# Local and pooled attention into a mixture of experts: a new order, a shorter pooling matrix, sums on a second engine

## The chip, the cores and the metric

One Trainium2 chip, one core of it. The metric is the device time of one execution in microseconds (us); lower is better. The runs of a kernel are given by their median.

## The reference, cut to what matters

Two layers, all in float32. The first works on 8 images (batch) x 8 heads, sequence 576, head size 64; the second on the result as 8 x 576 rows of 512 features, with 4 experts of 64 columns, of which each row uses 2.

```python
def _attn_ref(q, k, v):                       # factor = 4
    q_d, k_d, v_d = means over 4 neighbours of q, k, v        # 144 positions
    out_d = sm_attn(q_d, k_d, v_d)
    out_up = np.repeat(out_d, factor, axis=2)
    mask = np.abs(pos[:, None] - pos[None, :]) < factor       # a band of 7
    ...
    attn = attn / (np.sum(attn, axis=-1, keepdims=True) + 1e-09)
    out_local = np.matmul(attn, v)
    return out_up + out_local

def _moe_ref(x, w_gate, wq, wk, wv, wo):      # K = 2
    logits = x @ w_gate
    w = softmax over the two largest logits of a row
    for e in range(4):
        q, k, v = x @ wq[e], x @ wk[e], x @ wv[e]
        a = causal softmax of (q @ k.T) / 8
        ye = a @ v @ wo[e]
        out += w (where e is among the two) * ye
```

## The kernel before, in words

For each image b the kernel runs three stages; stages of neighbouring images overlap (image b's first stage runs beside the second of b-1 and the third of b-2).

Stage 1 works on pairs of heads c = 0..3 of image b. `load` (L475) brings q, k (128 x 584, transposed) and v (two loads of 64 rows, five windows of 128). `s1_local` (L493) makes ten tiles of local scores on TensorE (PE), L505, masks them on VectorE (DVE), L508, takes maxima, L511, subtracts them on GpSimd (POOL), L520, exponentiates on ScalarE (ACT), sums, L523, adds epsilon to the sum, L524 (`l_eps`), takes the reciprocal and normalises, L526, on POOL or DVE. `s1_down` (L530) pools q and k by four (`down4`: one reduction on DVE, L541, with a piece of 16 columns more for k, or two additions on POOL, L545), pools v, makes the pooled scores (L578), their maxima (`d_max`), the scaling of the maxima by 1/128 (`d_scl`, L583), the exponential (L588), the sum with epsilon (`d_eps`, L591) and the normalisation (`d_nrm`). v is pooled in two ways: for image 0 by matmuls with a pooling matrix `pool` (L563), for the other images by additions (`vd`, L557 and L558, POOL or DVE) on a second copy of v, `lr`, that comes with two loads of its own, a large one (L484, 256 KB) and a small one (L486, 64 KB: 16 rows of 2 KB, read twice, for the two halves of 32 partitions). `s1_out` (L614) transposes both softmax results (L361), evicts them (L316 on DVE, L314 on ACT), multiplies with v (L643 to L655), adds both parts into x (L663, on DVE) and splits x into a high and a low part, xh (L668, ACT) and xl (L669). x(b,c) below is the result of pair c of image b.

Stage 2 projects x to q, k (L686; L701 for the first q) and v with the gate's logits (L732, L741), each as three products of high and low parts. Stage 3 makes causal scores by rows of two tiles (L845), maxima (L865), exponentials (L868), the sum with epsilon (`s_eps`, L872), the reciprocal (L873), the normalisation with the gate's weight (`s_nrm`, L876), transposes, products with v (L959) and the output projection (L982, L1004).

The order of the work is written out by hand as a list. Each operation that the functions above declare with `op(name, engines, cost, ...)` has a number; SEQ (L17 to L158) lists the numbers in the order in which the operations are issued. An entry x stands for operation x // 4, and x % 4 says which of the operation's engines does it: "GV" with remainder 0 is POOL, with 1 DVE. An entry -1 is a warming matmul on zeros (`filler`, L463), whose result nothing reads. There are 22 of them, and seven more at the start (L343). Each engine, and the queue of SyncE (SP) that issues all DMAs, does its part of the list strictly in order.

Buffers are slots of pools. In `load`, q and k have NLD = 2 slots each and v has NLV = 2, so the load of pair 2 waits until the last reader of pair 0 is through: for q the local scores and the pooling, for v the product with v. A load that waits holds all that stand behind it on SP. The tags "q" (NQ = 3 slots) and "k" (NK = 2) hold the projected q and k of stage 3, "xh" and "xl" (8 slots each) the two parts of x.

`constants` (L391) makes the pooling matrix `pool` (128 x 7 x 128): entry (row, k, column m) is 1 where the row's position lies in the group of four that column m stands for. It counts positions less four times the column with six counters on POOL (L398, L400; 704 columns in all), compares with 0 on DVE (L405) and with 3.5 (L410, L412), the second comparison multiplied by the first. `own` masks rows that belong to another window.

## Time and profile before

| | us |
|---|---|
| median of 3 runs | 457.26 (456.78 to 457.70) |
| the profiled execution, its own time | 456.31 |
| its span, first to last instruction | 454.5 |
| busy: PE, DVE, ACT, POOL | 442.4 (97%), 373.5 (82%), 335.2 (74%), 303.8 (67%) |

The profiled execution's time is 1.8 us more than its span (what lies around the first and last instruction), and 0.95 us less than the median of the runs. Busy time of PE is modelled at the ends of matmuls, so a full PE in a stretch says that a matmul follows a matmul, not that none could be faster. Idle time of an engine counts only where something behind it waits.

### The profile page before, as it was taken

To read this page: it belongs to the slowest core of one execution; us is meant where nothing else is said; L and a number is where in the kernel's file an instruction comes from. 1 tells how busy PE (TensorE), PEld (TensorE's weight loads), DVE (VectorE), ACT (ScalarE), POOL (GpSimd) and SP (SyncE) were. 2 spreads that over 40 slices of the span, in tenths; PEclk is the share of its full clock that TensorE was granted. 3 is DMA by queue.
4 is the path that set the end of the run, shared out by engine and by line. 5 is a ranking of instruction groups with operands and counts; after the bars stand their busy time and mean duration, and the time that the engine had idled before them with its cause. 6 is when DMAs were issued, how large, how long until landed. Compare 5 with 4: busy or idle time off the path is not lost.

```text
span 454.5 us, 20339 instructions
## 1 busy us (share of the span) xinstructions
PE 442.4 (97%) x8373; PEld 400.6 (88%) x8373; DVE 373.5 (82%) x1099; ACT 335.2 (74%) x1056; POOL 303.8 (67%) x447
## 2 busy tenths in 40 slices
PE   8889999999999999999999999999999999999997
PEld 3768998989999889999999898999898998999876
DVE  7989999899968999777889999996897658466782
ACT  2988797876968988766866886675997688366873
POOL 7789779769757988755893888855687861024340
PEclk9999999999999999999999999999999999999999
DMA  8787455343415542624354253333352200110112
GB/s 246 233 231 188 128 168 173 88 147 100 133 48 169 179 129 72 190 85 112 105 152 158 85 126 82 126 112 99 117 162 81 74 1 3 53 53 14 48 61 105
DMA packets 43460, 52.70 MB, mean 116 GB/s; under 512 B 3304, under 2 KB 26344, under 8 KB 43368
## 3 DMA queue, kind: packets, MB, share of 16 engines
q1 hardware_dynamic: 43368, 51.40, 38.1%
q8 instruction: 66, 1.08, 1.0%
q14 instruction: 26, 0.21, 0.2%
HBM read 40.90 MB, written 9.44 MB: 111 GB/s over the span
## 4 chain that ended last, share of the span: by engine, by line
PE 81%; DVE 10%; ACT 3%; issue 2%; DMA 2%; POOL 1%; SPq 0%; DVEq 0%; POOLq 0%; ACTq 0%
PE pj L686 20%; PE po L982 10%; PE sq L845 9%; PE pv L732 8%; PE o L959 8%; PE tq L361 5%; PE tp L361 4%; PE o L643 3%; PE sc L505 3%; PE scd L578 2%; PE pv L741 2%; PE po L1004 1%; PE o L650 1%; DMA lk<-in_kT_dram 1%; DMA lv<-in_v_dram 1%
## 5 line engine op out<-in xcount | busy, mean ns | idle before, releaser
L876 POOL TENSOR_SCALAR pr<-pr,pst,gt 128x128 f32<-128x128 f32 (+8 forms) x101 | 71.5, 718 | 51.3 <-DVE pst L873 33.0
L868 ACT ACTIVATE pr<-pr,pst 128x448 f32<-128x448 f32 (+8 forms) x144 | 79.9, 558 | 11.7 <-DVE pst L865 11.1
L686 PE MATMUL pj<-xh,wqk_h 128*128 128x320 f32 (+1 forms) x248 | 75.1, 303 | 0.0
L686 PE MATMUL pj<-xl,wqk_h 128*128 128x320 f32 (+1 forms) x248 | 73.2, 295 | 0.2 <-issue 0.2
L686 PE MATMUL pj<-xh,wqk_l 128*128 128x320 f32 (+1 forms) x248 | 72.9, 294 | 0.0
L865 DVE CUSTOM_DVE_ANT_0 pr<-sq,causal_t 128x448 f32<-128x448 f32 (+8 forms) x144 | 64.1, 484 | 5.1 <-PE sq L845 4.9
L845 PE MATMUL sq<-k,q 64*64 64x256 f32 (+6 forms) x768 | 51.8, 371 | 0.5 <-ACT k L314 0.5
L686 PEld LDWEIGHTS pj<-xh,wqk_h 128*128 128x128 f32 x248 | 46.6, 188 | 3.3 <-issue 1.1
L686 PEld LDWEIGHTS pj<-xh,wqk_l 128*128 128x128 f32 x248 | 46.6, 188 | 0.0
L686 PEld LDWEIGHTS pj<-xl,wqk_h 128*128 128x128 f32 x248 | 46.6, 188 | 0.0
L588 ACT ACTIVATE dp<-scd,dst 128x144 f32<-128x144 f32 x96 | 35.1, 375 | 9.9 <-DVE dst L583 7.3
L845 PEld LDWEIGHTS sq<-k,q 64*64 64x64 f32 x768 | 32.9, 133 | 7.9 <-ACT k L314 0.7
L526 POOL TENSOR_TENSOR lp<-lp,lst 128x640 f32<-128x640 f32 x25 | 32.4, 1294 | 8.5 <-DVE lst L525 6.0
L732 PE MATMUL pv<-wvg_h,xh 128*128 128x260 f32 x128 | 36.9, 288 | 0.2 <-ACT dp L588 0.2
L669 POOL TENSOR_TENSOR xl<-x,xh 128x576 fp32r<-128x576 f32 x23 | 32.8, 1425 | 5.1 <-ACT xh L668 5.1
L732 PE MATMUL pv<-wvg_l,xh 128*128 128x260 f32 x128 | 36.2, 283 | 0.0
L732 PE MATMUL pv<-wvg_h,xl 128*128 128x260 f32 x128 | 36.0, 282 | 0.0
L982 PE MATMUL po<-oh,wo_h 128*128 128x256 f32 (+1 forms) x112 | 34.0, 304 | 0.0
L971 POOL TENSOR_TENSOR ol<-oc,oh 128x256 fp32r<-128x256 f32 (+1 forms) x27 | 22.4, 830 | 16.2 <-ACT oh L970 16.0
L982 PE MATMUL po<-oh,wo_l 128*128 128x256 f32 (+1 forms) x112 | 32.9, 294 | 0.0
L982 PE MATMUL po<-ol,wo_h 128*128 128x256 f32 (+1 forms) x112 | 32.9, 294 | 0.0
L361 PE MATMUL tq<-ident,pr 64*128 64x64 f32 x736 | 32.3, 227 | 0.5 <-DVE ptb L316 0.5
(181 smaller groups left out, 1432.1 us busy)
## 6 DMA issues: line engine op xcount, KB each, us to landing
lv<-in_v_dram SPq DMA_DIRECT2D x64, 160.0 KB
lq<-in_qT_dram SPq DMA_DIRECT2D x32, 292.0 KB
lk<-in_kT_dram SPq DMA_DIRECT2D x32, 292.0 KB
out_dram<-ot SPq DMA_DIRECT2D x28, 288.0 KB
lr<-in_v_dram SPq DMA_DIRECT2D x28, 256.0 KB
lr<-in_v_dram SPq DMA_DIRECT2D x28, 64.0 KB
wst<-in_wqk_dram SPq DMA_DIRECT2D x1, 1024.0 KB
vx<-vg SPq DMA_DIRECT2D x8, 128.0 KB
```

Source lines behind the costliest of these rows:

```text
L361: T.transpose(ps()[:, 512 * x + z[x]:512 * x + z[x] + 64], data[r, 0:128], ident[r, r])
L526: op("l_nrm", "GV", (pool_tt(n), dve(n)), lambda e: eng[e].tensor_tensor(p(), p(), st[:, :, 2:3].to_broadcast([128, NT, W]), op=OP.mult), ...
L588: A.activation(p()[:, t, :], scs()[:, at * t:at * t + SD], AF.Exp, bias=st[:, t, 4:5], scale=1.0 / 128.0, accum_out=st[:, t, 0:1])
L669: op("xl", "GV", (1360, dve(576)), lambda e: eng[e].tensor_tensor(xl(), x(), xh()[:, 0:S].bitcast(F32), op=OP.subtract), r=[x, (xh, 0)], w ...
L686: T.matmul(ps()[:, H0 + n0:H0 + n1], ww[:, c, w0 + 128 * p:w0 + 128 * p + 128], xx[b, c]()[:, n0:n1], start=(i == 0), stop=(i == 3 * NP - 1))
L732: T.matmul(ps()[:, at:at + 260], xx[b, c]()[:, 128 * t:128 * t + 128], ww[:, c, :], start=(i == 0), stop=(i == 3 * NP - 1))
L845: T.matmul(pss[x][0]()[halves[e ^ turned(t)], at_of[x] + at + to:at_of[x] + at + to + n1 - n0], q()[r, 64 * t:64 * t + 64], k()[r, n0:n1], ...
L865: op("s_max", "V", dve(n) + 4, lambda x=x, t=t, n=n, src=src: V.tensor_tensor_reduce(rows_of[t], src(), causal_t[:, S - 64:S + 256] if t = ...
L868: op("s_exp", "A", 281 + n / 1.2, lambda x=x, t=t, n=n: A.activation(rows_of[t], rows_of[t], AF.Exp, bias=st[:, x, 4:5], scale=-1.0, accum ...
L876: op("s_nrm", "GV", (327 + n / 1.2 + max(0, n - 384) * 1.1, 189 + n / 1.92), lambda g, x=x, t=t, n=n: eng[g].tensor_scalar(rows_of[t], row ...
L959: T.matmul(obs[x]()[r, q0:q1], vg()[kr, j, 64 * (2 * p + e):64 * (2 * p + e) + 64], pt()[kr, e, j, q0:q1], start=j == 0, stop=j == len(job ...
L982: T.matmul(ps()[:, H1 + n0:H1 + n1], ww[:, p, 128 * c:128 * c + 128], xx[b, p]()[:, n0:n1], start=(i == 0), stop=(i == 5))
```

## The change

1. SEQ is new: 2591 entries for 2561, with 24 warming matmuls for 22. PE's part of the list has the same operations; from 80 us on they stand in the old order but for neighbours and near neighbours that change places. At the start the eleven warming matmuls before and after the first local tile are gone, and ten stand behind the first pooled scores. DVE's, ACT's and POOL's parts are new throughout. SP issues q and k of pairs 0 to 3 of image 0 ahead of most of v.
2. Sums with epsilon may go to POOL, as one addition of two columns; 49 of 128 do (24 `s_eps`, 15 `d_eps`, 10 `l_eps`). The scaling `d_scl` may go to ACT; 20 of 32 do. Pooling of q and k in image 1 and `d_nrm` in images 0 and 1 may now choose their engine as elsewhere. Over the whole list the engines of other operations change too, among them three more of the pooled values `vd` on DVE (13 for 10), six fewer poolings of k on POOL (11 for 17), three fewer xl on DVE (6 for 9), seven fewer evictions `tp_ev` on DVE (13 for 20).
3. Pairs 2 and 3 of image 0 are loaded into slots of the tags "q", "k" and "xh".
4. The pooling matrix comes from a row of column numbers (128 columns), and, for each row and each of the seven k, one number: the position shifted right by two, as a float. Column m belongs to the row where both are equal.
5. The small load of `lr` is two loads of 16 partitions each, each with one reading of the rows. This makes 28 more DMAs.

```diff
-    1152, 36, 2100, 20, 0, 193, -1, -1, -1, -1, -1, 4, 8, 16, 156, 196, -1, 32, 144, 292, 40, 140, 84, 88, 96, -1,
...
+    44, 0, 20, 24, 1168, 192, 2132, 32, 4, 156, 16, 197, 28, 208, -1, 212, 217, 36, -1, 140, 144, 292, -1, -1, -1,
...
+    def add_eps(e, dst, st):
+        if e == "G":
+            G.tensor_tensor(dst, st[:, :, 0], st[:, :, 1], op=OP.add)
+        else:
+            V.tensor_reduce(dst, st[:, :, 0:2], op=OP.add, axis=AX.X)
+
...
     def constants():
-        cks = [buf(wk, [128, n], "ck", 8, I32, tag="xh") for n in (512, 192)]
-        ges = [buf(wk, [128, n], "ge", 8, tag="xl") for n in (512, 192)]
+        row, at = buf(wk, [128, 128], "row", 8, I32, tag="xh"), buf(wk, [128, 2, 8], "at", 8, I32, tag="xl")
...
         def count():
+            G.iota(row(), pattern=[[1, 128]], base=0, channel_multiplier=0)
...
-                for ck, z0, z1, k0 in ((cks[0], 0, 512, 0), (cks[1], 0, 128, 4)):
-                    G.iota(ck()[r, z0:z1].rearrange("p (k m) -> p k m", m=128), pattern=[[TQ, (z1 - z0) // 128], [-4, 128]],
-                           base=TQ * k0 - PADL - 4 * WT + SH * x, channel_multiplier=1)
-                G.iota(cks[1]()[r, 128:192].rearrange("p (k z m) -> p k z m", z=2, m=WT), pattern=[[TQ, 2], [0, 2], [-4, WT]],
-                       base=-PADL + SH * x, channel_multiplier=1)
-
-        def above():
-            for x, n0, n1, own_x in ((0, 0, 512, 0), (1, 0, 128, 1), (1, 128, 192, 0)):
-                V.tensor_scalar(ges[x]()[:, n0:n1], cks[x]()[:, n0:n1], 0.0, own[:, own_x:own_x + 1], op0=OP.is_ge, op1=OP.mult)
+                G.iota(at()[r, 0, 0:5], pattern=[[TQ, 5]], base=SH * x - PADL - 4 * WT, channel_multiplier=1)
+                G.iota(at()[r, 0, 5:7], pattern=[[TQ, 2]], base=SH * x - PADL, channel_multiplier=1)
+
+        def group():
+            V.tensor_scalar(at()[:, 0, 0:7], at()[:, 0, 0:7], 2, None, op0=OP.arith_shift_right)
+            V.tensor_copy(at()[:, 1, 0:7].bitcast(F32), at()[:, 0, 0:7])
...
         def fill_pool():
-            flat = pool.rearrange("p k m -> p (k m)")
-            for x, n0, n1 in ((0, 0, 512), (1, 512, 640)):
-                V.scalar_tensor_tensor(flat[:, n0:n1], cks[x]()[:, 0:n1 - n0], 3.5, ges[x]()[:, 0:n1 - n0], op0=OP.is_lt, op1=OP.mult)
-            z = [t()[:, 128:192].rearrange("p (k m) -> p k m", m=2 * WT) for t in (cks[1], ges[1])]
-            V.scalar_tensor_tensor(pool[:, 5:7, 64 - WT:64 + WT], z[0], 3.5, z[1], op0=OP.is_lt, op1=OP.mult)
+            for k in range(7):
+                dst, src = (pool[:, k], row()) if k < 5 else (pool[:, k, 64 - WT:64 + WT].rearrange("p (z m) -> p z m", m=WT), strided(row()[:, 0:WT], (0, 2)))
+                own_x = own[:, 1:2] if k == 4 else own[:, 0:1]
+                V.tensor_scalar(dst, src, at()[:, 1, k:k + 1].bitcast(F32), own_x, op0=OP.is_equal, op1=OP.mult)
...
         def masks():
...
-        op("c_cnt", "G", 2100, count, w=cks, alloc=cks)
-        op("c_ge", "V", 740, above, r=cks, w=ges, alloc=ges)
-        op("c_pool", "V", 1430, fill_pool, r=cks + ges, w=[(PL, 1)])
+        op("c_cnt", "G", 1000, count, w=[row, at], alloc=[row, at])
+        op("c_ge", "V", 300, group, w=[at])
+        op("c_pool", "V", 1250, fill_pool, r=[row, at], w=[(PL, 1)])
...
     def load(b, c):
-        q = LQ[b, c] = buf(ld, [128, SP], "lq", NLD)
-        k = LK[b, c] = buf(ld, [128, SP], "lk", NLD)
-        vw = LV[b, c] = buf(ld, [128, 5, 128], "lv", NLV)
+        if b == 0 and c >= NLD:
+            q, k = buf(wk, [128, SP], "lq", NQ, tag="q"), buf(wk, [128, SP], "lk", NK, tag="k")
+            vw = buf(wk, [128, 5, 128], "lv", 8, tag="xh")
+        else:
+            q, k = buf(ld, [128, SP], "lq", NLD), buf(ld, [128, SP], "lk", NLD)
+            vw = buf(ld, [128, 5, 128], "lv", NLV)
+        LQ[b, c], LK[b, c], LV[b, c] = q, k, vw
...
-            op("load", "D", 220, lambda: nc.sync.dma_start(vr[64 - WT:64 + WT, 1], bass.AP(
-                tensor=v.tensor, offset=raw, ap=[[0, 2], [512, WT], [1, 512]])), w=[(VR, 1)])
+            for x in range(2):
+                op("load", "D", 220, lambda x=x: nc.sync.dma_start(vr[64 + WT * (x - 1):64 + WT * x, 1], bass.AP(
+                    tensor=v.tensor, offset=raw, ap=[[512, WT], [1, 512]])), w=[(VR, 1 + x)])
...
-        op("l_eps", "V", 90, lambda: V.tensor_reduce(st[:, :, 2], st[:, :, 0:2], op=OP.add, axis=AX.X), w=[ST])
+        op("l_eps", "VG", (90, 190), lambda e: add_eps(e, st[:, :, 2], st), w=[ST])
...
-        def down4(name, dst, src, more=0, engs="V" if VB <= b < B0 else "GV"):
+        def down4(name, dst, src, more=0, engs="GV"):
...
-        op("d_scl", "V", 72, lambda: V.tensor_scalar(
+        op("d_scl", "VA", (72, 210), lambda e: A.mul(st[:, :, 4], scs()[:, 1000:1003], 1.0 / 128.0) if e == "A" else V.tensor_scalar(
...
         def ex():
...
-        op("d_eps", "V", 70, lambda: V.tensor_reduce(st[:, :, 2], st[:, :, 0:2], op=OP.add, axis=AX.X), w=[ST])
+        op("d_eps", "VG", (70, 190), lambda e: add_eps(e, st[:, :, 2], st), w=[ST])
...
         def norm(e):
...
-        if b < B0:
-            op("d_nrm", "A", 921, lambda: norm("A"), r=[ST], w=[p])
-        else:
-            op("d_nrm", "GVA", (pool_tt(432), dve(432), 921), norm, r=[ST], w=[p])
+        op("d_nrm", "GVA", (pool_tt(432), dve(432), 921), norm, r=[ST], w=[p])
...
-        op("s_eps", "V", 70, lambda: V.tensor_reduce(st[:, 0:m, 2], st[:, 0:m, 0:2], op=OP.add, axis=AX.X), w=[ST])
+        op("s_eps", "VG", (70, 190), lambda e: add_eps(e, st[:, 0:m, 2], st[:, 0:m]), w=[ST])
```

## Rows read from the trace of the kernel before

us are counted from the span's start.

**Rows 1.** Windows: us, then busy us of each engine (instructions), PE's clock, DMA share, GB/s.

```profile
5.00:20.00 15.00, 13.58 (x289) 9.76 (x291) 14.16 (x34) 9.18 (x35) 10.54 (x19) 1.00 0.91 266
20.00:40.00 20.00, 17.20 (x475) 14.09 (x470) 17.07 (x47) 17.39 (x55) 18.57 (x21) 1.00 0.82 229
40.00:80.00 40.00, 39.58 (x810) 36.56 (x811) 38.25 (x99) 32.87 (x109) 32.83 (x44) 1.00 0.54 156
80.00:440.00 360.00, 357.17 (x6662) 329.05 (x6663) 295.35 (x897) 267.87 (x844) 235.56 (x337) 1.00 0.34 100
```

**Rows 2.** Waits of DVE, 0 to 45 us: us in total, times, longest.

```profile
DVE lp L508 <- PE scd L578: 2.1, 1, 2.1
```

**Rows 3.** Waits of PE, 0 to 45 us, the row on v.

```profile
PE pv L563 <- DMA lv<-in_v_dram: 1.0, 2, 0.6
```

**Rows 4.** Waits of SP's queue, 0 to 80 us, the longest.

```profile
SPq L489 <- PE o L655: 11.9, 5, 5.1
```

**Rows 5.** Chain that ended last, 0 to 60 us: start, us, what.

```profile
23.88 4.94 DMA lv<-in_v_dram
```

**Rows 6.** Timeline of DVE, 40 to 45 us: start, us, instruction, where x(0,3) is made.

```profile
41.33 0.74 DVE L663 SCALAR_TENSOR_TENSOR x<-up,o 128x576 f32<-128x576 f32 x1
```

**Rows 7.** Timeline of DVE, 7 to 13 us, the pooling matrix.

```profile
7.40 1.08 DVE L405 TENSOR_SCALAR ge<-ck,own 128x512 f32<-128x512 int32 x3
9.64 2.22 DVE L410 SCALAR_TENSOR_TENSOR pool<-ck,ge 128x512 f32<-128x512 int32 x2
11.78 0.21 DVE L412 SCALAR_TENSOR_TENSOR pool<-ck,ge 128x64 f32<-128x64 int32 x1
```

**Rows 8.** Groups of instructions, DVE: form, count, busy us, mean ns, idle before.

```profile
L583 DVE TENSOR_SCALAR dst<-scd 128x3 f32<-128x3 f32 x32 | 5.1, 158 | 0.5
L524 DVE TENSOR_REDUCE lst<-lst 128x10 f32<-128x20 f32 x32 | 5.4, 168 | 0.4
L316 DVE COPY vd<-pv 128x256 f32<-128x256 f32 x2 | 0.8, 414 | 0.0
L316 DVE COPY pd<-tp 128x480 f32<-128x480 f32 x14 | 9.1, 653 | 5.3 <-PE tp L361 5.2
L526 DVE TENSOR_TENSOR lp<-lp,lst 128x640 f32<-128x640 f32 x7 | 7.1, 1015 | 0.0
```

**Rows 9.** Groups by form, 0 to 13 us, line 405.

```profile
L405 DVE TENSOR_SCALAR ge<-ck,own 128x128 f32<-128x128 int32 x1 | 0.4, 445 | 0.0
L405 DVE TENSOR_SCALAR ge<-ck,own 128x64 f32<-128x64 int32 x1 | 0.2, 244 | 0.0
```

**Rows 10.** Groups of instructions, POOL and ACT.

```profile
L777 POOL TENSOR_TENSOR gw<-cm 128x20 f32<-128x20 f32 x8 | 1.8, 222 | 0.6
L794 ACT ACTIVATE cm<-cm 128x20 f32<-128x20 f32 x8 | 1.8, 219 | 1.1 <-POOL cm L777 1.1
L876 POOL TENSOR_SCALAR pr<-pr,pst,gt 128x128 f32<-128x128 f32 (+8 forms) x101 | 71.5, 718 | 51.3 <-DVE pst L873 33.0 <-PE o L963 6.9 <-PE po L982 4.1
```

**Rows 11.** Line 486, its DMA issues on SP: duration ns min/median/max, first and last start.

```profile
L486 SPq DMA_DIRECT2D lr<-in_v_dram x28: 640/677/761, 23.1 to 339.9; - x28
```

**Rows 12.** Timeline of PE, 1 to 7 us.

```profile
1.17 3.17 PE L343 MATMUL wu<-zero 128*128 128x512 bf16 x7 [1.17 <-DVE zero L340]
5.78 0.81 PE L505 MATMUL sc<-lk,lq 64*64 64x64 f32 x40
```

**Rows 13.** Groups of instructions, DVE, pooling of v.

```profile
L557 DVE TENSOR_TENSOR lr<-lr 128x512 f32<-128x512 f32 x10 | 8.3, 829 | 0.0
L558 DVE TENSOR_TENSOR vd<-lr 128x256 f32<-128x256 f32 x10 | 6.5, 654 | 0.3
```

**Rows 14.** Timeline of POOL, 72 to 81 us, the low part of x(1,3).

```profile
76.48 1.42 POOL L669 TENSOR_TENSOR xl<-x,xh 128x576 fp32r<-128x576 f32 x1 [0.54 <-ACT xh L668]
```

**Rows 15.** Chain that ended last, 70 to 90 us: the projections.

```profile
80.22 3.17 PE pj L686 x24
83.40 2.84 PE pv L732 x24
```

279 rows, old and new, of the table SEQ are left out of this document.

## The prediction

> **What bounds the kernel now.** The reading starts with the table of busy time by stretch [rows 1]. From 80 to 440 us TensorE (PE) is busy 357.17 of 360 us: there the kernel is its matmuls, one behind the other, and 2.8 us of holes are all that any reordering can win. Before 80 us it is different. From 5 to 20 us VectorE (DVE) is busy 14.16 of 15 us while PE, whose 13.58 us are partly warming matmuls, waits for it; from 20 to 40 us PE is idle for 2.8 us and DVE for 2.9; from 40 to 80 us both are full (39.58 and 38.25 of 40). So a microsecond that DVE gives back before about 42 us brings everything behind it forward, if the stretch from 40 to 80 us does not swallow it. The waits say what the holes between 20 and 40 us are: DVE once sits 2.1 us before the mask of a local tile, until PE gets to it [rows 2], and PE waits 1.0 us for a v tile [rows 3]. That tile was late because its load stood in SyncE's (SP's) queue: SP spent 11.9 us before v loads, until PE's o matmuls had read the previous tile in the slot [rows 4], and the chain of waits runs through the load itself, issued at 23.88 and 4.94 us long [rows 5].
>
> The milestone that I use is x(0,3), the last of the four results of image 0; in the trace before it is DVE's 72nd planned operation and ends at 41.33 + 0.74 = 42.07 [rows 6], and v and k projections of image 0 follow it.
>
> **Pooling matrix.** Removed from DVE are the three comparisons of L405, the two of L410 and the one of L412: 1.08 + 2.22 + 0.21 = 3.51 us [rows 7]. New are two operations on 7 columns (0.16 each, as the three-column one of L583 [rows 8]), five on 128 columns and two on 32. No row has the new form with a comparison for equality. The nearest are L405's 0.445 us for 128 columns and 0.244 for 64 [rows 9], one tensor in and a per-partition operand, as the new ones. Upper end: 0.32 + 5 x 0.445 + 2 x 0.244 = 3.03; lower end, with 0.244 for the wide and 0.16 for the narrow ones: 1.86. The 0.445 cannot be all work, since four times its width took 0.1 us more in the same group; I take the middle, 2.4. That is -1.1 us (-1.65 to -0.5) for DVE. The shorter counters on POOL take away about 1 us at 2 us, when DVE is still in its setup: nothing.
>
> The same rows show what a second input costs: L410 has counter and comparison as inputs, and its pair takes 2.22 us where L405's three, with more columns and one tensor in, took 1.08 [rows 7]. The Trainium skill (SBUF — State Buffer, "Who interferes with whom") has a rule for it: a VectorE instruction with two SBUF inputs contends with a GpSimd one that reads SBUF, and whichever is second is blocked. [...]
>
> **Small operations.** The numbers of the new order choose the engine by their remainder. Of the 128 sums with epsilon, 49 go to POOL (24 of the causal scores, 15 of the pooled ones, 10 of the local ones) and 20 of 32 scalings go to ACT. Up to x(0,3) DVE loses four sums (0.168 each, as the local one), four scalings (0.158 each) and two copies of pooled v (0.414 each), and gains one copy of a transposed tile (0.653) and one normalisation (1.015) [rows 8]; a pooled k stands in for a pooled q, which I put at +0.2 for its extra piece of 16 columns. That is -2.1 + 1.9 = -0.2 us. On POOL such a sum takes about 0.22 us, on ACT about 0.22 [rows 10], so over the whole run POOL gets 49 x 0.22 = 11 us and ACT 20 x 0.22 = 4.4 us; from 80 to 440 us they are busy 236 and 268 of 360 [rows 1], and have room. What could cost is not their length but their place: POOL works in order, and a sum may stand behind a normalisation of 0.72 us [rows 10]. On the path I take 0; it is the rival below.
>
> **Other buffers for pairs 2 and 3.** Their q, k and v no longer wait for the slots of pairs 0 and 1, so the two loads of q and k and the v loads go out at once. The DMA engines were nearly full (0.91 of their time from 5 to 20 us [rows 1]), so they deliver as fast as they can: the gain is that nothing stands still in SP's queue. What can be won is the two holes, 2.1 and 1.0 us [rows 2, 3]; it cannot be less than 0 except through contention. Part of the first hole is PE's own order, which is chosen anew. I take half, -1.5 us (-3.1 to 0).
>
> **Split of the small load.** One issue of 0.68 us on SP [rows 11] becomes two. If each is as long, SP has 28 x 0.68 = 19 us more of 454; if each is half, nothing. SP is waiting for slots in this phase and not for its own time [rows 4], so 0; without that cover each pair's pooled v would be 0.7 us later.
>
> **Order at the start.** The new order has none of the eleven warming matmuls that stood before and after the first local tile. The seven of the setup took 3.17 us for 7 x 512 columns, 0.45 each, which is the 1.2 GHz level; the first local tile's 40 matmuls took 0.81 us after them and five more warming ones [rows 12]. If the first tile now runs at the lower level, it takes at most twice that, +0.8 us. It also starts up to 1.3 us earlier, and DVE first pools k, makes the matrix and takes a maximum before it reads this tile: 0 on the path. Two more warming matmuls in all (24 for 22) lie in PE's holes; at most 2 x 0.45.
>
> **From 40 to 80 us.** Here the change gives DVE work back: three pooled v tiles of image 1 that POOL had (0.829 + 0.654 each [rows 13]) less some small operations, about +2.9 us between x(0,3) and x(1,3). So x(1,3) may come hardly earlier than before. Cover: its second half was done at 76.48 + 1.42 = 77.90 [rows 14], and the q projection of image 1 that reads it began at 80.22; the new order puts one v operation, 12 matmuls or 2.84 / 2 = 1.4 us, ahead of that projection [rows 15]. PE, 2.8 us early, would be there at 80.22 - 2.8 + 1.4 = 78.8, still behind 77.9. So 0, by 0.9 us; without the cover up to +1.4.
>
> **After 80 us** PE's order is the old one but for neighbours that change places, with the same matmuls. Holes of 2.8 us may close or others open: 0 (-2.8 to +3). The last stores end as before.
>
> **Sum:** -1.1 - 0.2 - 1.5 = -2.8 us. The profiled execution took 456.31 us, 0.95 below the median of 457.26. From the profiled one comes 453.5; from the median, which is what is timed, 454.5 us.
>
> **Rivals.** *Given back.* DVE is the bound until 80 us, and what it saves before 42 us it gets back as pooled v tiles; if the cover of 0.9 us is not there, since DVE also loses time to POOL's reads, x(1,3) holds PE and -2.8 becomes about -0.3 +- 0.8: 457.0. For it: 38.25 of 40 us busy. Against it: PE stood nowhere in that stretch for long.
> *Slower: the sums on POOL.* Place: the softmax chains between 80 and 440 us, where PE has no slack. A sum that stands behind one normalisation waits half of 0.72, say 0.4 us with the hand-over, and the reciprocal, the scaling and the transpose wait with it. If 12 of the 49 do so with PE waiting, +4.8 against -2.8: 459.3. It decides from 7 of 49 on (7 x 0.4 = 2.8). Against it: POOL sat idle for 33 us just before such normalisations, until a reciprocal came from DVE [rows 10], so it is often free when the sum is due. The Trainium skill (Perfetto Trace Analysis, "Optimizing Scalar/DVE Operations") speaks on its side: moving operations from VectorE to GpSimd may not help, because they share a read port.
> *More than the sum.* Both holes between 20 and 40 us close (-3.1), the matrix is at its lower end (-1.65), and DVE's relief later closes a third of the holes after 80 us (-1): with the -0.2 that is -6, 451.3. For it: all three are single waits with a cause that the change touches.
> *A part does nothing.* The split load touches no wait of PE or DVE; I give it no time either way.
>
> **How the numbers follow.** Forecast 0.50, given back 0.18, slower 0.15, more 0.17. A measurement of this kernel tells about 0.2% (0.9 us) from no change. Faster by more than that: 0.50 + 0.17 and a third of the case given back, 0.73. Same: 0.11, from that case. Slower: 0.15 and the rest of it, 0.16. The likeliest case has its own range from 452.3 (matrix -1.65, holes -3.1, small -0.2) to 456.6 (-0.7). The range for 8 in 10 reaches down into "more" and up through "given back": 451.0 to 458.0.
>
> **What would show it.** Right: x(0,3) ends near 39.3 instead of 42.1, the q projection of image 1 starts near 79, DVE's wait for the local tile and PE's wait for v are gone, DVE's pooling matrix takes about 2.4 us, and PE from 80 us on is as full as before. Wrong: PE idle in the waits with POOL's sums or with x behind it between 60 and 80 us; more than 4 us of PE holes after 80 us; or the first 40 us unchanged, because loads or POOL (18.57 of 20 us busy from 20 to 40 [rows 1]) were the bound instead of DVE.

## The result, and the profile after

The changed kernel is **slower**: 460.66 us in the median of 17 runs (458.17 to 463.52), against 456.78 us (454.73 to 458.47) of 17 runs of the kernel before on the same chip. The ratio is 1.0082, with a 95% interval from 1.0062 to 1.0102, so 3.9 us. The prediction said 454.5, in a range from 451.0 to 458.0. The profiled execution took 463.52 us (span 461.7), the longest of its runs, with a mean granted clock of TensorE of 0.992. Of the 17 runs one had a mean granted clock of 1.00, nine 0.996, seven 0.991 to 0.993; of 23 runs of the kernel before (in the first set of experiments) fourteen had 1.00. Two single runs stood far off the others of their kernel (698.30 us with the new matrix, 1460.38 us with TensorE's old order, which is the profiled one): the medians and ratios below are without them, and nothing is read from the latter's trace.

Busy time by stretch, as in [rows 1]:

```profile
5.00:20.00 15.00, 12.73 (x209) 7.98 (x203) 13.93 (x31) 9.69 (x37) 10.40 (x18) 1.00 1.08 283
20.00:40.00 20.00, 16.33 (x364) 12.66 (x366) 12.49 (x27) 11.80 (x39) 12.65 (x18) 0.83 0.64 147
40.00:80.00 40.00, 38.53 (x814) 35.40 (x809) 39.22 (x97) 34.24 (x115) 31.46 (x42) 1.00 0.56 152
80.00:440.00 360.00, 357.69 (x6726) 330.68 (x6728) 292.20 (x846) 270.00 (x863) 238.43 (x363) 1.00 0.34 102
```

From 80 us on TensorE is as full as before (357.69 against 357.17): all is lost ahead of that. From 20 to 40 us it gets through 364 matmuls where it did 475 [rows 1], at a mean clock of 0.83, and VectorE is busy 12.49 instead of 17.07 us: it was not the bound there, it starved. The DMA engines went from 0.91 to 1.08 of their time in the 15 us before that (the share adds up the times of all packets, so it can pass 1). The waits of PE from 5 to 80 us (us in total, times, longest) and its timeline name the hole, as I call idle time of TensorE between two matmuls:

```profile
PE tp L368 <- issue: 3.3, 1, 3.3
PE sc L513 <- issue: 1.1, 1, 1.1
PE scd L586 <- DVE kd L551: 1.0, 1, 1.0
PE o L648 <- PE scd L586: 0.9, 1, 0.9
```

```profile
24.30 0.46 PE L368 MATMUL tp<-ident,lp 64*128 64x64 f32 x8
28.03 0.37 PE L368 MATMUL tp<-ident,lp 64*128 64x64 f32 x2 [3.27 <-issue]
28.33 2.32 PE L470 MATMUL wu<-zero 128*128 128x512 bf16 x4
30.58 1.33 PE L648 MATMUL o<-pt,lv 64*64 64x58 f32 x40
```

Eight of ten transposes of one tile run at 24.30, and the last two, with the same operands, 3.27 us later, with nothing that the profile shows to wait for ("issue"; what ended a wait is called its releaser). Behind the hole the clock is at its lower level (1.2 GHz): the 40 matmuls of L648 take 1.33 us, where the same form took 0.81 at 23.16. In the stretches around it (the last three columns are the granted clock, the DMA share and GB/s) the clock goes from 1.00 to 0.76 and 0.56:

```profile
20.00:25.00 5.00, 4.76 (x126) 4.13 (x126) 3.86 (x10) 2.89 (x7) 4.12 (x8) 1.00 1.13 230
25.00:30.00 5.00, 1.86 (x5) 0.52 (x6) 2.14 (x4) 1.56 (x6) 2.39 (x2) 0.76 0.79 165
30.00:35.00 5.00, 5.00 (x120) 4.08 (x118) 1.48 (x3) 3.64 (x15) 3.08 (x4) 0.56 0.05 11
```

A second, quieter loss lies ahead of it, in the timeline of PE:

```profile
11.48 0.81 PE L513 MATMUL sc<-lk,lq 64*64 64x64 f32 x40
12.22 1.69 PE L470 MATMUL wu<-zero 128*128 128x512 bf16 x7
13.84 0.71 PE L586 MATMUL scd<-kd,qd 64*64 64x144 f32 x12
14.48 0.39 PE L470 MATMUL wu<-zero 128*128 128x512 bf16 x1
14.71 1.72 PE L571 MATMUL pv<-lv,pool 128*128 128x128 f32 x14
```

The 14 pooling matmuls of pair 0 start at 14.71. In the kernel before they started at 11.43:

```profile
11.43 1.80 PE L563 MATMUL pv<-lv,pool 128*128 128x128 f32 x14 [0.44 <-DMA lv<-in_v_dram]
```

The new order puts eight warming matmuls and pair 1's pooled logits (its pooled scores) ahead of them. PE counts as busy here, so no list of waits shows this loss. With both losses x(0,3) ends at 47.32 + 0.75 = 48.07, not at 42.07 [rows 6]:

```profile
47.32 0.75 DVE L668 SCALAR_TENSOR_TENSOR x<-up,o 128x576 f32<-128x576 f32 x1
```

The waits that the prediction wanted gone are gone: PE's for v [rows 3], and SyncE's 11.9 us before v loads for the o matmuls [rows 4] are 1.0 us up to 60 us; VectorE's 2.1 us [rows 2] are 0.7 at the longest. The pooling matrix of [rows 7] is now

```profile
4.81 0.88 DVE L408 TENSOR_SCALAR at<-at 128x7 int32<-128x7 int32 x1
5.72 0.45 DVE L409 CAST at<-at 128x7 f32<-128x7 int32 x1
6.59 2.38 DVE L415 TENSOR_SCALAR pool<-row,at,own 128x128 f32<-128x128 int32 x7
```

3.71 us, against 3.51 before.

### The profile page after: what moved, and what is told of

It is laid out like the page before. It is cut to its first block, busy times and chain, and to the rows that moved or that the text cites. A ratio compares the mean times of both kernels' runs of the same rounds, so it can differ in the third digit from the quotient of the medians.

```text
span 461.7 us, 20335 instructions
## 1 busy us (share of the span) xinstructions
PE 447.1 (97%) x8374; PEld 403.6 (87%) x8375; DVE 371.2 (80%) x1046; ACT 338.9 (73%) x1086; POOL 302.2 (65%) x475
## 3 DMA queue, kind: packets, MB, share of 16 engines
q8 instruction: 66, 1.08, 1.0%
## 4 chain that ended last, share of the span: by engine, by line
PE 91%; DVE 3%; issue 2%; ACT 2%; DMA 1%; POOL 0%; SPq 0%; DVEq 0%; ACTq 0%; POOLq 0%
PE pj L691 21%; PE pv L737 10%; PE po L987 10%; PE sq L850 9%; PE o L964 8%; PE tq L368 6%; PE tp L368 5%; PE sc L513 4%; PE o L648 4%; PE scd L586 3%; PE pv L746 2%; PE o L655 2%; PE wu L470 2%; PE po L1009 1%; PE o L968 1%
## 5 line engine op out<-in xcount | busy, mean ns | idle before, releaser
L873 ACT ACTIVATE pr<-pr,pst 128x320 f32<-128x320 f32 (+8 forms) x144 | 79.8, 556 | 17.3 <-DVE pst L870 16.3
L881 POOL TENSOR_SCALAR pr<-pr,pst,gt 128x192 f32<-128x192 f32 (+8 forms) x101 | 66.2, 663 | 20.4 <-DVE pst L878 10.6
L674 POOL TENSOR_TENSOR xl<-x,xh 128x576 fp32r<-128x576 f32 x26 | 37.7, 1450 | 7.4 <-ACT xh L673 7.0
```

The source lines that it names most:

```text
L674: op("xl", "GV", (1360, dve(576)), lambda e: eng[e].tensor_tensor(xl(), x(), xh()[:, 0:S].bitcast(F32), op=OP.subtract), r=[x, (xh, 0)], w ...
L873: op("s_exp", "A", 281 + n / 1.2, lambda x=x, t=t, n=n: A.activation(rows_of[t], rows_of[t], AF.Exp, bias=st[:, x, 4:5], scale=-1.0, accum ...
L881: op("s_nrm", "GV", (327 + n / 1.2 + max(0, n - 384) * 1.1, 189 + n / 1.92), lambda g, x=x, t=t, n=n: eng[g].tensor_scalar(rows_of[t], row ...
```

## The experiments

All were timed against the kernel before on the same chip (its median was 456.2 to 457.0 in each set). Medians in us, ratios with 95% intervals (a ratio is taken over all runs of a set and is not the quotient of the two medians):

| kernel | median | ratio |
|---|---|---|
| before + other buffers | 457.52 | 1.0030 (1.0007 to 1.0054) |
| before + new matrix | 457.49 | 1.0028 (1.0006 to 1.0051) |
| before + new matrix, conversions later | 457.65 | 1.0024 (1.0001 to 1.0046) |
| the same, output weights' load later | 459.51 | 1.0061 (1.0033 to 1.0089) |
| before + split loads | 457.23 | 1.0009 (0.9980 to 1.0038) |
| before + split loads and moved small operations | 474.40 | 1.0388 (1.0350 to 1.0426) |
| before + extra copies | 460.94 | 1.0101 (1.0060 to 1.0142) |
| before + pooling matmuls later | 456.82 | 1.0021 (0.9991 to 1.0050) |
| start of before, rest of changed | 456.62 | 1.0003 (0.9976 to 1.0031) |
| start of changed, rest of before | 460.24 | 1.0091 (1.0058 to 1.0124) |
| changed, old buffers | 459.41 | 1.0070 (1.0044 to 1.0095) |
| changed, more warming | 461.11 | 1.0107 (1.0085 to 1.0130) |
| changed, old buffers and loads' order | 460.77 | 1.0096 (1.0069 to 1.0123) |
| changed, TensorE's old order at the start | 466.64 | 1.0205 (1.0176 to 1.0233) |
| the same, old buffers | 473.04 | 1.0352 (1.0323 to 1.0380) |
| changed, pooling matmuls earlier | 458.35 | 1.0029 (1.0007 to 1.0051) |
| the same, old buffers | 457.92 | 1.0015 (0.9986 to 1.0043) |

### Where the loss is: the start

```diff
 SEQ = (
-    (order of the changed kernel up to the first scores, 55 us)
+    (order, buffers and matrix of the kernel before up to there; the reverse in the second; split loads in both)
```

> The order, the engines, the buffers and the pooling matrix of the kernel before up to its first scores (55 us); from there on the order and engines of the changed kernel, with its split loads. Theory, from the two traces: everything that was lost lies before 50 us, and the new order behind it is as good as the old one or 1 us better. Then it takes 455 to 457 us, no more than the kernel before (456.3). Rival, the sums on GpSimd cost time in the softmax chains: 458 to 461 us.

> The complement: the changed kernel up to its first scores (order, engines, buffers, matrix), the order and engines of the kernel before behind it; the split loads stay. Theory: the loss is in the start, 459.5 to 462 us, with the hole without a releaser in the transposes at 23 to 28 us. Rival: 456 to 458 us.

456.62 and 460.24 us: the start alone carries the loss, and the new order behind it neither costs nor gives more than 0.3%.

### The buffers and the crowd of loads

```diff
-        if b == 0 and c >= NLD:
+        if False:
```

> The changed kernel with one part undone: q, k and v of pairs 2 and 3 are back in the two slots of the load pool, every order is kept. Theory 1, early loads: without slots to wait for, the loads keep the DMA engines full up to 28 us (share 1.06 to 1.13 in each 5 us up to 25), TensorE's next instructions come late (holes of 1.1 and 3.3 us before which no wait is shown), and the clock falls to 1.2 GHz behind them. Then this kernel has no hole over 1 us without a releaser between 18 and 30 us, a DMA share below 1.0 from 20 to 25 us, and takes 455 to 457.5 us. Theory 2, the new order of the engines' work at the start is slow by itself (the second image's first local tile stands behind more work): it stays at 460 to 461 us. Theory 3, the late warming: also 460 to 461 us, with the lower clock again.

459.41, a ratio of 1.0070 against 1.0082 for the changed kernel: 0.5 us less, with intervals that overlap. Most of the loss stays. The hole is down from 3.27 to 0.89 us; another, of 1.4 us, stands at 39.2.

The other way round, the buffers alone in the kernel before:

> The kernel before with the other buffers for pairs 2 and 3 alone; its order, pooling matrix and loads are kept. Theory 1: SyncE no longer waits 11.9 us before v loads, the DMA share from 20 to 30 us rises from 0.75 to over 0.95, holes without a releaser appear on TensorE before 30 us, and the time is 1 to 4 us over the kernel before. Theories 2 and 3: the two holes of 2.1 and 1.0 us shrink as predicted, and the time is 0 to 3 us under it.

1.2 us slower than before, and as theory 1 has it. The kernel before from 20 to 30 us, then this one, and its waits of PE:

```profile
20.00:30.00 10.00, 7.65 (x195) 5.79 (x187) 7.93 (x20) 8.80 (x29) 8.94 (x13) 1.00 0.75 219
```

```profile
20.00:30.00 10.00, 7.29 (x227) 5.87 (x223) 6.85 (x18) 8.33 (x29) 7.96 (x11) 0.90 1.06 224
```

```profile
PE pv L566 <- DMA lv<-in_v_dram: 2.4, 1, 2.4
PE tp L360 <- issue: 1.9, 1, 1.9
```

A wait on SyncE was removed, and two on TensorE came. My reading is that the loads of pairs 2 and 3 share the DMA engines with the v tile that pair 0 needs first, and with something that TensorE's transposes wait for without a semaphore. A crowd by itself, with no other edit:

```diff
+        if nj == 17 and o.eng == "D":
+            for x in range(4):
+                nc.sync.dma_start(junk[x], qT[7, x])
```

> The kernel before with four copies of 292 KB from DRAM to DRAM, which nothing reads, issued by SyncE at 15.6 us, where it stood idle before a v load until 20.3 us. Theory, full DMA engines delay TensorE's own instructions: the hole without a releaser in the transposes of the second pair's result, 0.77 us at 23.2 us in the kernel before, grows to 1.5 to 3.5 us, and the time by 1 to 4 us. Rival, the hole belongs to the order of the work: it stays below 1 us, and only the v load issued at 20.3 us lands later (0 to 1 us in all).

4.8 us slower on the medians, more than the whole loss of the changed kernel and than either side expected. But the hole in the transposes did not grow: it fell from 0.77 to 0.20 us, behind a wait of 1.17 us that ended with an eviction of ScalarE. The large one stands elsewhere:

```profile
PE pv L566 <- issue: 3.5, 1, 3.5
```

```profile
30.00:40.00 10.00, 7.15 (x136) 6.61 (x136) 5.81 (x17) 5.32 (x18) 5.05 (x5) 0.66 0.52 148
```

It is ahead of pooling matmuls, whose v tile SyncE issued at 26.56 instead of 23.88 [rows 5]; the trace names no releaser, but the same matmuls waited for their v load in the kernel before [rows 3], and no instruction packet (below) landed in the 4.1 us ahead of their start. So the run shows that a crowd costs this much, and again with the clock at its lower level behind the hole, but by a late load and not by late instructions. That the hole in the transposes belongs to the instructions comes from where it stands:

```diff
+ TensorE: 5 warming matmuls
  TensorE: local logits, pair 0
+ TensorE: 6 warming matmuls
```

> The changed kernel with eleven warming matmuls put back around its first local tile (five ahead, six behind). Theory 3, that the lower clock at the start costs the time: local(0,0) takes 0.8 instead of 1.34 us, the later steps come forward, 457 to 459 us. Theory 1: the hole of about 3 us in the transposes of the second pair's result and the low clock behind it stay, 460 to 461.5 us. Theory 2: 460 to 462 us.

461.11: late warming was not it, although the first local tile again took 0.81 us. The hole remained (3.04 us), but no longer in the transposes: it stood in the matmuls ahead of them. Counted from the start, the place is the same. Busy time from 0 to a point within the hole, for the kernel before, the changed one, this one and the one with old buffers (the count behind PE's busy time is that of its matmuls so far):

```profile
0.00:23.70 23.70, 20.22 (x345) 12.92 (x345) 21.01 (x56) 14.34 (x46) 18.35 (x51) 1.00 0.81 239
```

```profile
0.00:26.00 26.00, 21.14 (x344) 13.50 (x345) 22.11 (x60) 14.08 (x45) 18.33 (x51) 1.00 1.00 252
```

```profile
0.00:25.00 25.00, 20.90 (x345) 12.96 (x346) 21.30 (x57) 13.88 (x45) 17.88 (x51) 1.00 0.99 262
```

```profile
0.00:23.90 23.90, 20.32 (x345) 12.71 (x345) 21.25 (x59) 14.09 (x45) 16.91 (x50) 0.93 0.75 220
```

TensorE stops after its 345th matmul, whatever that is: a transpose in three of them, an o matmul in the fourth (the second trace lacks one record). Five more runs have the hole at that count. Its length goes with the DMA share, from the start on and more clearly in the 5 us before TensorE stops:

| kernel | DMA share from 0 | share in the last 5 us | hole, us |
|---|---|---|---|
| before | 0.81 | 0.83 | 0.77 |
| changed, old buffers | 0.75 | 0.85 | 0.89 |
| before + split loads | 0.82 | 0.85 | 1.04 |
| start of before, rest of changed | 0.85 | 0.94 | 1.18 |
| before + other buffers | 0.98 | 1.09 | 1.95 |
| start of changed, rest of before | 0.98 | 1.10 | 2.62 |
| changed, more warming | 0.99 | 1.10 | 3.04 |
| changed, pooling matmuls earlier | 1.00 | 1.11 | 2.22 |
| changed | 1.00 | 1.12 | 3.27 |

Seven runs had no hole over 0.3 us there, with a share of 0.21 to 0.55 in those 5 us: the new matrix and its two variants, the old order of loads, split loads and moved small operations, and the two last ones with old buffers in the table of runs. The kernel before with later pooling matmuls had 0.41 us at 0.64. Only the run with the copies does not fit: 0.20 us at 1.03. The DMA queues hold instruction packets too; this is the changed kernel from 24.76 to 28.03 us:

```profile
q1 hardware_dynamic: 602, 0.57, 89.9%
q14 instruction: 2, 0.02, 3.0%
q8 instruction: 1, 0.02, 2.8%
```

The packet of queue 8 has 16 KB. It started at 24.90 us, 0.14 us after TensorE had stopped, landed at 26.38, and TensorE went on 1.65 us later; in the kernel before it started at 21.55, 1.7 us ahead of the stop. The traces have 52 holes of TensorE over 0.3 us without a releaser, at any time of the run, and 51 of them end 1.2 to 1.7 us after a packet of this queue has landed; the one of 3.5 us in the run with the copies is the exception, and there the 346th matmul also came 1.4 us after such a landing. My reading is that TensorE's next instructions come in these packets, over the same DMA engines as the loads, and queue with them. The constant count, the table and the landings speak for it; what a packet holds the trace does not say.

### The order of the loads

```diff
-        if b == 0 and c >= NLD:
+        if False:
...
-            for x in range(2):
+            (one load of the small rows, as before)
...
+ SyncE: the first 42 loads in the order of the kernel before
```

> The changed kernel in its own order on the four computing engines, with the old buffers, the unsplit small load and the order in which the kernel before issues its first 42 loads. Theory, the loads (their crowd and their order) make the loss: 455.5 to 457.5 us, no hole without a releaser over 1 us, no low clock behind one. Rival, the order of the computing engines makes part of it: 458.5 to 460 us, as with the old buffers alone (459.4).

460.77, above both ranges and on the rival's side: the old loads do not heal the changed kernel. They are late for its own order:

```profile
PE pv L562 <- DMA lv<-in_v_dram: 3.9, 1, 3.9
```

Loads and matmul order are tuned to each other, which the next two runs show more sharply.

### TensorE's order

```diff
- TensorE: the changed order up to the first scores
+ TensorE: the order of the kernel before up to there
```

> The changed kernel with one engine's order undone in the start: TensorE's, up to the first scores, is that of the kernel before (with its warming matmuls); the other engines, the buffers and the loads stay. In the changed order the pooling matmuls of the first pair stand behind seven warming matmuls and the logits of pair 1, at 14.8 instead of 11.4 us, and the first result ends 3.7 us later. Theory A, TensorE's new order makes what the buffers don't: 457.5 to 459 us, the rest being the crowd of early loads. Theory B, the order of VectorE, ScalarE and GpSimd makes it: 460 to 462 us, TensorE waiting for them where it now warms.

> The same with the old buffers for pairs 2 and 3 as well. Theory A, TensorE's order and the crowd make the loss together: 455.5 to 457.5 us, as the kernel before. Theory B, the order of the other engines: 458.5 to 460.5 us, as with the old buffers alone (459.4).

466.64 and 473.04 us; both theories were wrong. One engine's old order beside the other engines' new ones is worse than either kernel. It leaves the question open, and only a small move can answer it:

```diff
  TensorE: local logits, pair 1
+ TensorE: pooling matmuls, pair 0 (14)
- TensorE: 7 warming matmuls
  TensorE: pooled logits, pair 1
  TensorE: 1 warming matmul
- TensorE: pooling matmuls, pair 0 (14)
```

> The changed kernel with one move: the 14 pooling matmuls of pair 0 stand right behind pair 1's local logits, and the seven warming matmuls that stood there are gone. If that place in TensorE's order is what costs, they start at 12.2 to 12.7 us instead of 14.8, the first result is up to 2 us earlier, and the time is 458 to 460 us. If they only waited beside something that is late anyway: 460 to 461.5 us.

458.35: of the 3.9 us, 2.4 are back (0.82% became 0.29%, and the intervals do not touch). The matmuls start at 11.14, and wait for nothing but 0.60 us of VectorE:

```profile
9.72 0.81 PE L507 MATMUL sc<-lk,lq 64*64 64x64 f32 x40
11.14 1.80 PE L565 MATMUL pv<-lv,pool 128*128 128x128 f32 x14 [0.60 <-DVE lst L513]
```

(The local logits ahead of them were earlier as well in this execution, by 1.8 of the 3.6 us; the ten warming matmuls before them took 0.23 us each, where eight of them took 0.34 us each in the changed kernel's execution. That part is not due to the move.) The run undoes two things at once, the place and the seven warming matmuls, and no run separates them in this order. The hole of 2.22 us is still there. With the old buffers too:

> The changed kernel with the one move of the first pooling matmuls and with the old buffers for pairs 2 and 3. Theory, two causes that add: the place of these matmuls (2.4 us, from 460.7 to 458.35) and the early loads (1.2 us, as in the kernel before). Then 456 to 457.8 us, no slower than the kernel before (457.0), and the hole ahead of TensorE's instructions at 24 us falls from 2.2 to under 1.2 us. Rival, the buffers no longer matter once the matmuls are moved: 458 to 459 us.

457.92 us, ratio 1.0015, an interval that includes 1: the two parts undone, the loss can no longer be told from none. There was no hole over 0.7 us ahead of 30 us without a releaser; the waits that are left are those for operands:

```profile
PE scd L580 <- DVE kd L545: 1.6, 1, 1.6
PE tp L362 <- ACT dp L590: 1.2, 1, 1.2
```

The gain of the buffers here, 0.43 us (0.14% by the ratios), is itself within the uncertainty; that they matter rests on the kernel before, where they cost 1.2 us. The reverse move in the kernel before:

```diff
  TensorE: local logits, pair 1
- TensorE: pooling matmuls, pair 0 (14)
  TensorE: pooled logits, pair 1
+ TensorE: 1 warming, pooling matmuls, pair 0 (14)
```

> The kernel before with the reverse move alone: the 14 pooling matmuls of pair 0 stand behind pair 1's pooled logits, as in the changed kernel. Theory: they start at 13.5 to 14.5 instead of 11.4 us, the first result comes 1 to 2 us later, and the time is 457.5 to 459 us against 457.0. Rival, the place matters only beside the changed order of VectorE and ScalarE: 456.5 to 457.2 us.

456.82, ratio 1.0021: unclear, although the pooling matmuls started at 13.37 instead of 11.43. Without the seven warming matmuls and beside the old order of VectorE the place costs less than can be told.

### The parts that the prediction priced

The matrix by itself:

```diff
-        op("c_ge", "V", 740, above, r=cks, w=ges, alloc=ges)
-        op("c_pool", "V", 1430, fill_pool, r=cks + ges, w=[(PL, 1)])
+        op("c_ge", "V", 300, group, w=[at])
+        op("c_pool", "V", 1250, fill_pool, r=[row, at], w=[(PL, 1)])
```

> The kernel before with the new pooling matrix alone (shorter counters on GpSimd, seven comparisons for equality on VectorE). By the prediction VectorE's matrix falls from 3.51 to 1.9 to 3.0 us, and what lies behind comes forward by 0.5 to 1.65 us: 455 to 456.5 us against 456.8 before. If VectorE is not what holds the start, 456.8 as before; if the seven comparisons cost more than the six operations that they replace, over 457.

The seven comparisons took 2.53 us and the two small ones 0.16 + 0.17: 2.86, so 0.65 less than 3.51, within the bounds. The time was 1.20 us worse, not better. VectorE's row, and the wait of ScalarE from 5 to 20 us:

```profile
8.69 2.53 DVE L407 TENSOR_SCALAR pool<-row,at,own 128x128 f32<-128x128 int32 x7
```

```profile
ACT wvg_h L449 <- DMA wst<-in_wvg_dram: 9.2, 1, 9.2
```

ScalarE's first work is to convert weights whose load was issued at 3.5 us in both kernels and landed 1.9 us later here (the wait was 7.3 us before), and the first exponentials stand behind it. VectorE then waited 1.16 us for them. So in this execution it is a load that ends last, and VectorE's gain is no gain. Why the load landed later no run shows: in six kernels with the old matrix and the same first loads ScalarE waited 7.3 to 8.3 us for it. And in the trace of the kernel before the load did not end last, for behind the conversions ScalarE waited for VectorE's scaling:

```profile
ACT dp L588 <- DVE dst L583: 1.3, 1, 1.3
```

With the conversions moved behind the exponentials:

```diff
+ ScalarE: first exponentials, pair 0
  ScalarE: 4 conversions of the gate and value weights
- ScalarE: first exponentials, pair 0
+ VectorE: scaling for these exponentials, ahead of the matrix
+ GpSimd: the 4 low parts of the same weights together, ahead of the pooling of pair 2
```

> The kernel before with the new pooling matrix, and with ScalarE's conversions of the gate and value weights moved behind its first exponentials (and the scaling that these need ahead of the matrix on VectorE). With the matrix alone ScalarE stood until 11.4 us before the weights' load, 1.9 us longer than in the kernel before, and the time was 457.5 us. Theory, loads and not VectorE set the end of the first 15 us: VectorE's wait of 1.16 us for the first exponentials goes, and the time is 454.5 to 456.5 us. Rival, the matrix gives nothing wherever it stands: 457 to 458 us.

457.65: VectorE's wait is gone, and nothing is won. But the low parts on GpSimd, of which three stood later in the old order, behind other work, now wait for the conversions together and take 2.86 us in one go, ahead of work for pair 0 (waits of POOL, 5 to 20 us):

```profile
POOL wvg_l L451 <- ACT wvg_h L449: 2.3, 1, 2.3
```

PE then stood 2.1 us before a transpose for a normalisation of GpSimd. That is a cost of the run's own order, so it leaves open what the matrix gives where no load holds ScalarE. The same kernel with a later load:

```diff
- SyncE: load of the output weights at place 18
+ SyncE: load of the output weights at place 31
```

> The kernel with the matrix and the moved conversions, and with the load of the output weights (512 KB) moved from SyncE's 18th to its 31st place, 10 us later, so that the DMA engines are less full when TensorE's instructions are due at 21 to 23 us. Theory of late instructions: the hole ahead of TensorE's 346th matmul, 0.77 us in the kernel before, falls under 0.5, and the time is 0 to 1 us under the kernel with the matrix and the conversions alone, 453.5 to 456 us. Rival: no difference between the two.

459.51, wrong: ScalarE waited 2.2 us for this load, and PE 1.3 us for ScalarE. A lighter DMA load at 21 us was paid for at 40.

The small operations and the split:

```diff
-        op("l_eps", "V", 90, lambda: V.tensor_reduce(st[:, :, 2], st[:, :, 0:2], op=OP.add, axis=AX.X), w=[ST])
+        op("l_eps", "VG", (90, 190), lambda e: add_eps(e, st[:, :, 2], st), w=[ST])
...
+    (the engines of the changed kernel for 69 of these, in the order of the kernel before)
```

> The kernel before in its own order, with the small operations on the engines that the changed kernel gives them (sums on GpSimd, scalings on ScalarE) and the split small loads. Prediction: nothing for either, 455.5 to 457 us. If a sum that stands behind a normalisation on GpSimd makes TensorE wait, or the 28 more loads make SyncE late: 458 to 461 us.

> The kernel before with the split small loads alone (28 more loads of 32 KB). The kernel with the split and the small operations on other engines took 474.4 us against 456.2. If the small operations make all of that (a sum on GpSimd stands there in a queue that was not ordered for it), this one takes 455.5 to 457.5 us. If the loads make it, since SyncE is late for those of the later images, 470 us and more.

474.40 with both, 457.23 with the split alone: the moved small operations, 49 sums and 20 scalings together, cost 17 us in an order that was not made for them. PE from 80 to 440 us, and the longest waits of GpSimd and of VectorE for GpSimd there, with both:

```profile
80.00:440.00 360.00, 347.62 (x6434) 318.09 (x6438) 283.64 (x796) 256.36 (x818) 235.97 (x369) 1.00 0.33 98
```

```profile
POOL pst L316 <- ACT pr L871: 33.1, 10, 9.4
DVE pst L876 <- POOL pst L316: 7.8, 11, 1.7
```

A sum of 0.2 us at the head of GpSimd's queue waits up to 9.4 us for the exponentials, and everything behind it waits as well. GpSimd waited as long in the kernel before, ahead of its normalisations (33.0 us [rows 10]); new is that VectorE waits for GpSimd's sums, here and in two more groups (7.3 and 5.5 us). How much of the 17 us is due to the scalings on ScalarE no run separates. The changed kernel has such waits of GpSimd too (24.9 us), but VectorE waits only 2.5 us for sums of this group, and PE is busy for 357.69 us: its order has put behind them what is not needed yet.

## Why the prediction was wrong

**Order at the start, "0 on the path": this step failed, and it is the largest part of the loss.** The prediction looked at the first local tile alone, and priced a lower clock for it at 0.8 us at most (it took 1.34 instead of 0.81 in the profiled execution, and putting the warming back won nothing). It did not follow PE's list on to the first pooling matmuls, which stand 3.3 us later behind warming that no wait shows. Moving them back, without seven of the warming matmuls, gave 2.4 of the 3.9 us. The place was put at nothing without a reason: what PE's later steps were moved behind was not looked at.

**Other buffers, -1.5 us, which "cannot be less than 0 except through contention": the sign was wrong.** The exception was the case. The prediction read the DMA share of 0.91 [rows 1] as "they deliver as fast as they can", and SyncE's 11.9 us [rows 4] as time lost. Those waits left the DMA engines room: without them the share from 20 to 30 us rose from 0.75 to 1.06. In the kernel before these buffers alone cost 1.2 us; PE waited 2.4 us for v, and the hole at the 345th matmul grew from 0.77 to 1.95 us. In the changed kernel the cost is within the uncertainty (0.12 and 0.14% in two pairs of runs). The two holes that were to be won did close there.

**Pooling matrix, -1.1 us (-1.65 to -0.5): mis-sized, and not found in the time.** Alone it measured -0.65; in the changed kernel, beside GpSimd's work, +0.2, since the two operations on 7 columns took 1.33 us, not 0.32. In the old order the time rose by 1.2 us all the same. The step counted on PE waiting for VectorE and left out the weights' load, which ended last in that run's trace; why it was late, and whether VectorE's gain would show without it, stays open. On the contention of two-input operations that the Trainium skill names (SBUF — State Buffer, "Who interferes with whom"), no run decides. Why an operation of 0.16 us, with one input, took 0.88 beside GpSimd's work at 4.8 us was not tried.

**Small operations 0, split 0, after 80 us 0: these held** for the new order, to the 0.3% that the run with the old start can tell. The rival that put its price on GpSimd's sums did not happen, because the order avoids it, but its mechanism is real: with the scalings, 17 us in the old order. The sentence of the Trainium skill (Perfetto Trace Analysis, "Optimizing Scalar/DVE Operations") that moving operations from VectorE to GpSimd may not help is borne out there, through the queue; that a shared port had part in it is not shown.

**From 40 to 80 us, 0:** PE lost about 1 us more than before (38.53 against 39.58 busy), most of it in the wait of 0.9 us of o matmuls behind L586, near 75 us; a minor miss. The prediction's own mark for being wrong, "the first 40 us unchanged, because loads ... were the bound", pointed at the right place: they did not stay the same, they became worse.

In sum, of the 0.82%: 0.53 came back with the place of the pooling matmuls (2.4 us), 0.14 more with the old buffers (within the uncertainty; alone in the kernel before they cost 0.30%), and 0.15 stayed, which cannot be told from none. What could not be settled is how the first two divide in a single execution, since the place of the matmuls also decides what the loads collide with. None of the versions beat the kernel before.

## What to carry to other kernels

A queue that waits for a slot is not lost time when the DMA engines behind it are at 0.9 of their time: its waits space the loads out, and what they leave free may carry things that no semaphore shows, as the packets of instructions do by my reading. When an order is chosen anew, compare each engine's list by where the first step of the longest chain stands, warming matmuls included, since an engine that warms counts as busy. And price a moved operation by what stands behind it in its new queue, not by its length: 69 operations of about 0.2 us cost 17 us here in one order and, as far as can be told, nothing in another.

## What the runs showed of the hardware that I had not expected

TensorE paused after its 345th matmul in nine of these kernels, in most in the middle of a group of equal instructions, for 0.77 to 1.18 us where the DMA share had been 0.83 to 0.94 in the 5 us before, and for 1.95 to 3.27 us at 1.09 to 1.12; at 0.21 to 0.55 seven kernels had no such pause. These pauses, and all but one of the others without a releaser, ended 1.2 to 1.7 us after a 16 KB packet of an instruction queue had landed. And what a pause costs is more than its length: in the changed kernel the two stretches of 5 us behind it had a granted clock of 0.76 and 0.56, the lower of the two levels (1.2 GHz) for most of them, although PE was busy throughout the second; in the kernel with the extra copies the 10 us behind 30 us had 0.66.
